# V's global rows straight into the copies' buffer, prices of the queue, jobs set into waits, and a first block in chunks of two tiles

## The chip, the cores and the metric

The kernel runs on one core of a Trainium2 chip. TensorE (PE in the profile, with PEld for its weight loads) multiplies matrices, VectorE (DVE), ScalarE (ACT) and GpSimd (POOL) work on elements, and SyncE (SP) issues the DMAs of this kernel in the order of its queue. The metric is the device time of one execution in microseconds (us): 894.03 us as the median of three runs, from 889.8 to 896.12.

## What is computed

Attention with a window, then two gated feed-forward blocks. The six weight matrices come as float64 and are turned into pairs of float16 parts on the chip; the rest is float32. There are 4 batches and 8 heads with 512 local and 32 global rows of 64 each:

```python
k_all = np.concatenate([k_g, k_l], axis=2); v_all = np.concatenate([v_g, v_l], axis=2)
out_g = np.matmul(sm(scale * np.matmul(q_g, k_all.transpose(0, 1, 3, 2))), v_all)
s_ll  = np.where(np.abs(pos[:, None] - pos[None, :]) <= 32, scale * q_l @ k_l.T, -1e9)
s_l   = np.concatenate([scale * q_l @ k_g.T, s_ll], axis=-1)
out_l = np.matmul(sm(s_l), v_all)
x  = np.concatenate([out_g, out_l], axis=2)          # as 2176 tokens x 512
xn = x / np.sqrt(np.mean(x * x, -1, keepdims=True) + 1e-6) * rms_g
x  = (silu(xn @ w_gate) * (xn @ w_val)) @ w_out      # 512 x 1536 and back
out = (sigmoid(x @ w2_gate) * (x @ w2_val)) @ w2_out
```

(Each local row sees the 32 global rows and the local ones at most 32 away; "@" with transposes is written short here.)

## The kernel before

**Attention.** The local rows are 16 tiles T of 128 rows, four to a batch. Per tile, q and k are loaded and transposed on PE (steps `q`, `k`), scores are made (`a1`, two score banks), the smallest is taken (`mx`, DVE), exponentials follow (`ex`, ACT), they are transposed (`a2`, PE), copied (`pc`) and multiplied with V (`a3`, 64 small matmuls per tile), normalized (`nm`), scaled (`sq`, `ms`, `sc`), split into two float16 parts in the tile `xs` (`xh`, `xm`) and sent by a transposing DMA to `xhi`, the input of the feed-forward block (`xl`, on SP). Once per batch the global rows go through `sg`, `g1`, `g2`, `g3`, `gx`.

**V's copies.** `a3` reads V from one of two buffers `vw0`, `vw1` (line 856; tile T uses `vw[T % 2]`), each with four blocks of rows: the row blocks that a 32-row strip of queries can see, and the global rows in the place that is left. `vw_pieces` (line 903) lists the copies of a tile: two large ones of 64 partitions, four small ones of 32, and for the first two tiles of a batch four more with the global rows. The buffer may only be written when `a3` of tile T-2 has read it. V's tile `vt` (six buffers) and V's global rows `vg` are loaded by `load_v` and `load_vg` (line 889), the latter four times into four strips of one tile; `st_vw` makes the copy on POOL, DVE, or as a DMA within SBUF on SP. A column of ones stands behind every head's 64 columns for the sum of the weights.

**Feed-forward.** The 17 row tiles (16 local, one of all global rows) go through block g=0 and g=1 of `w_gate`, `w_val` and `w_out` in chunks: `first` (line 1314) lists them as six chunks of three tiles (the last of two), that is of 384 columns and one of 256. A chunk takes 48 matmuls for gate and value (called GV here) when its tiles' `xl` have landed, and 24 for the output (OUT) one chunk later. Later blocks work on all rows at once and come after the attention.

**What sets the order.** The program is written by a list scheduler in the kernel itself. Every operation is a `task` with engines, a priority out of the table `PR` (line 1198) and the tasks that it depends on; `Booked` (line 88) prices each instruction as it is written, on a clock per engine in `now`, and `choose` (line 1435) takes the engine that is free first by these prices. A DMA's price on SP stands in line 123: 1250 ns for a transpose, 620 or 560 for others. `attend` (line 1493) runs this as long as attention tasks are left, with the chunks' matmuls as `G` pieces between them (`gemm`, line 1362); if PE has a gap of more than `fill` ns by these prices, it writes dummy matmuls on `ident` into it. From then on the order is that of the loops at the end, and `give` hands out conversion of weights and other side jobs to DVE, ACT and POOL at every `tick`. Nearly all instructions are recorded by the helper in line 145, so the rows of the profile carry that line and are told apart by their tiles.

Of the kernel before, what the change touches and what calls it, by code (L numbers as in the profile page):

```python
# [10 lines left out]
F32 = mybir.dt.float32  # L11
# [10 lines left out]
def tile_attention_moe_moe(  # L22
# [64 lines left out]

    class Booked:
# [4 lines left out]
        def __getattr__(self, name):  # L93
            f = getattr(self.eng, name)

            def g(*args, **kw):
# [3 lines left out]
                ins = [x for x in aps if x is not out]  # L100
                n = max(int(np.prod(x.shape[1:])) for x in aps) if "axis" in kw else int(np.prod(out.shape[1:]))
# [11 lines left out]
                elif key == "s":  # L113
# [9 lines left out]
                    now["s"] = t + (1250 if kw.get("transpose") else 620 if ns[0] < 100000 else 560 + 0.11 * min(max(now["dma"] - t, 0), 6000))  # L123
# [56 lines left out]
    SG = q_g.shape[2]  # L180
# [909 lines left out]
    def st_xh(T, e):  # L1090
        xs_t[T] = ap.tile([128, 2, DM], F16, tag="xs", name="xs", bufs=1)
# [42 lines left out]
    def st_g3(b, e):  # L1134
# [3 lines left out]
        for r in range(5):  # L1138
            for pr in range(NPR):
# [3 lines left out]
                else:  # L1143
                    l, v = pt[0:SG, r, 32 * pr:32 * pr + 32], vg[0:SG, h * DV:h * DV + D]
# [47 lines left out]
    def warm(n):  # L1192
        p = bank()
        for i in range(n):
# [3 lines left out]
    PR = dict(lkg=-7.25, kgt=7.41, lqg=-1.98, qgt=3.21, gB=1.07, lk=-4.25, lq=-1.55, lv=-0.02, lg=-0.66,  # L1198
              q=3.87, qc=-16.93, k=0.24, k0=-8.51, nk=-2.48, kc=3.82, kc0=-0.72, a1=8.55, vw=0.09, e=2.04,
              mx=-5.17, ex=2.53, a2=-3.33, pc=-0.11, a3=-0.84, nm=-4.07, sq=15.55, ms=-7.09, sc=-0.86,  # L1200
              a4=-18.55, xh=5.81, xl=-8.54, sg=8.94, g=5.82, lv0=-0.76, lk1=-6.39, G=1000, post=-7.94,
              raw=-3.21, w0=0.24, w1=0.35, w2=12.08, w3=16.91, w4=17.64, w5=-6.83, w6=7.76, w7=26.25,
              w8=11.55, Le=146, Ld=62, La=106, Lp=5314538, Ls=1690, backlog=4477, fill=1035, guard=1, kcd=0,
              land=1190, vs0=24309, vs1=341, vs2=1815, xt=0.37)
# [27 lines left out]
    def tile_tasks(T):  # L1232
# [6 lines left out]
        if t == 0:  # L1239
            task(("lg", b), "s", lambda e: load_vg(b), P(PR["lg"]),  # L1240
                 *([("vw", T - 8 + i, n) for i in range(2) for n in range(6, 10)] + [("g3", b - 2, 1)] if b >= 2 else []), after=ref("lg", b - 1))
# [32 lines left out]
        task(("xh", T), "ad", lambda e: st_xh(T, e), P("xh"), ("sc", T), ref("xl", T - 1), c=(520, 341))  # L1274
# [20 lines left out]

    def build_tasks():
        for n, a, dst in (("kg", k_g, kgT), ("qg", q_g, qgT)):
# [12 lines left out]
        task(("xh", NT), "ad", lambda e: st_xh(NT, e), NT, ("sc", NT), ref("xl", NT - 1), c=(520, 341))  # L1310
# [359 lines left out]
```

## Time and profile before

| | us |
|---|---|
| median of three runs | 894.03 |
| the profiled execution | 896.37 |
| its span, first to last instruction | 894.5 |
| PE busy in the span | 866.8 |
| DVE, ACT, POOL busy | 610.6, 452.2, 266.7 |

The profile is of one execution. Its span is 1.9 us shorter than the time of that execution, which is 2.3 us over the median of the runs. [...] The attention stage fills about the first 180 us.

### The profile page before, as it was taken

The page shows a single profiled execution, that of the slowest core. Times are in us where ns is not written, and L with a number is a line of the kernel's source. Part 1 is how long each engine was busy: PE and PEld are TensorE (multiplying, and loading weights), DVE is VectorE, ACT ScalarE, POOL GpSimd, SP SyncE. Part 2 cuts the span into 40 slices and gives each one's busy share as a digit, 9 for nine tenths or more (in the row PEclk, how much of TensorE's full clock was granted, in tenths as well). Part 3 has the DMA queues.
Part 4 walks back from the last instruction along what each step waited for, and adds up shares of the span by engine and source line. Part 5 has one row for each costly group of instructions (what it writes and reads, how often), then busy time and mean ns, then how long its engine had stood idle before and what let it go on. Part 6 is the DMA issues. An engine that isn't in the chain of part 4 may idle for free.

```text
span 894.5 us, 18832 instructions
## 1 busy us (share of the span) xinstructions
PE 866.8 (97%) x7733; PEld 543.3 (61%) x7733; DVE 610.6 (68%) x1050; ACT 452.2 (51%) x986; POOL 266.7 (30%) x300
## 2 busy tenths in 40 slices
PE   8889798899999999999999999999999999999998
PEld 6667565666666666666666666556556565556553
DVE  4867767697788888788737877748764468645252
ACT  4886586565334445555527444546545264344230
POOL 2754445342211211121214446442202122212010
PEclk9999999999999999999999999999999999999999
DMA  9977879461000114131300121110331003000102
GB/s 211 170 153 145 172 151 185 117 139 63 1 25 23 50 46 124 54 107 48 95 1 1 56 88 48 48 48 28 114 106 37 1 24 95 1 1 13 59 33 98
DMA packets 108998, 66.56 MB, mean 74 GB/s; under 512 B 76912, under 2 KB 101488, under 8 KB 108912
## 3 DMA queue, kind: packets, MB, share of 16 engines
q1 hardware_dynamic: 108912, 65.36, 29.2%
q8 instruction: 61, 1.00, 0.5%
q14 instruction: 25, 0.20, 0.1%
HBM read 52.17 MB, written 4.46 MB: 63 GB/s over the span
## 4 chain that ended last, share of the span: by engine, by line
PE 80%; DMA 9%; DVE 4%; ACT 2%; SPq 1%; issue 1%; POOL 1%; DVEq 0%; ACTq 0%; POOLq 0%
PE p L145 66%; PE b L145 14%; DMA vt<-in_v_l_dram 3%; DMA xhi<-xs 2%; DMA q<-in_q_l_dram 1%; DMA vw<-vt 1%; SPq L145 1%; DVE wf L145 1%; DVE xs L145 1%; DMA k<-in_k_l_dram 1%; ACT s L145 1%; DMA vg<-in_v_g_dram 1%; DVE ya L145 0%; ACT pt L145 0%; DVE wc L145 0%
## 5 line engine op out<-in xcount | busy, mean ns | idle before, releaser
L145 PEld LDWEIGHTS <-wc 128*128 128x128 f16 x2556 | 250.1, 98 | 144.8 <-issue 1.4
L145 PE MATMUL p<-tt,wc 128*128 128x384 f16 (+1 forms) x1296 | 208.6, 317 | 0.6 <-ACT gv L145 0.4
L145 PE MATMUL p<-xhi,wc 128*128 128x384 f16 (+1 forms) x1260 | 205.2, 317 | 0.0
L145 POOL TENSOR_TENSOR h<-gv,h 128x384 f16<-128x384 f32 (+1 forms) x66 | 84.4, 1279 | 286.1 <-ACT h L145 274.1
L145 PE MATMUL p<-wo,h 128*128 128x512 f16 x612 | 133.4, 379 | 0.0
L145 ACT ACTIVATE gv<-p 128x384 f32<-128x384 f32 (+1 forms) x174 | 80.4, 469 | 76.0 <-PE p L145 69.6
L145 DVE SCALAR_TENSOR_TENSOR wf<-raw,wf 128x512 int32<-128x512 int32 x144 | 113.2, 794 | 2.2
L145 PEld LDWEIGHTS <-wo 128*128 128x128 f16 x864 | 84.3, 98 | 47.7 <-issue 0.2
L145 PEld LDWEIGHTS <-h 128*128 128x128 f16 x612 | 59.9, 98 | 71.1
L145 DVE SCALAR_TENSOR_TENSOR ya<-p,ya 128x384 f32<-128x384 f32 (+2 forms) x106 | 61.0, 581 | 54.7 <-PE p L145 53.9
L145 PE MATMUL b<-xhi,wgv 128*128 128x384 f16 (+1 forms) x576 | 93.3, 320 | 2.0 <-DMA xhi<-xs 2.0
L145 ACT ACTIVATE h<-gv 128x384 f16<-128x384 f32 (+3 forms) x93 | 54.7, 592 | 73.5 <-DVE gv L145 71.2
L145 DVE SCALAR_TENSOR_TENSOR gv<-gv 128x384 f32<-128x384 f32 (+3 forms) x81 | 66.7, 823 | 36.2 <-ACT gv L145 35.3
L145 PE MATMUL p<-h,wo 128*128 128x384 f16 (+1 forms) x576 | 90.0, 317 | 0.0
L145 DVE TENSOR_TENSOR gv<-p,gv 128x384 f32<-128x384 f32 (+1 forms) x108 | 55.4, 530 | 46.8 <-ACT gv L145 46.6
L145 PEld LDWEIGHTS <-wgv 128*128 128x128 f16 x576 | 56.2, 99 | 34.6 <-issue 1.8
L145 ACT ACTIVATE sa<-p 128x384 f32<-128x384 f32 (+1 forms) x54 | 24.7, 466 | 79.2 <-PE p L145 79.0
L145 ACT ACTIVATE wf<-raw 128x512 f32<-128x512 f32 x72 | 47.2, 671 | 27.9 <-DVE wc L145 13.5
L145 POOL COPY vw<-vt 64x1040 f32<-64x1040 f32 (+1 forms) x37 | 39.5, 1069 | 50.2 <-DMA vt<-in_v_l_dram 38.7
L145 POOL TENSOR_TENSOR sm<-wf 128x256 f32<-128x256 f32 x18 | 15.4, 858 | 119.9 <-DVE wc L145 87.3
L145 POOL TENSOR_TENSOR hlo<-t,hhi 128x384 f16<-128x384 f32 (+1 forms) x24 | 26.6, 1109 | 69.3 <-ACT hhi L145 69.1
L145 PE MATMUL b<-hhi,wo 128*128 128x384 f16 (+1 forms) x192 | 46.9, 317 | 0.0
(117 smaller groups left out, 1007.1 us busy)
## 6 DMA issues: line engine op xcount, KB each, us to landing
raw<-in_moe_w_gate_dram SPq DMA_DIRECT2D x24, 512.0 KB, 4.1
raw<-in_moe_w_val_dram SPq DMA_DIRECT2D x24, 512.0 KB, 3.7
raw<-in_moe_w_out_dram SPq DMA_DIRECT2D x24, 512.0 KB, 3.7
k<-in_k_l_dram SPq DMA_DIRECT2D x16, 256.0 KB, 3.9
q<-in_q_l_dram SPq DMA_DIRECT2D x16, 256.0 KB, 4.9
vt<-in_v_l_dram SPq DMA_DIRECT2D x16, 256.0 KB, 5.3
out_dram<-ya SPq DMA_DIRECT2D x16, 256.0 KB, 2.0
vw<-vt SPq DMA_DIRECT2D x54, 65.0 KB, 2.8
```

Of the source, the lines that this page charges most:

```text
L145: return f(*args, **kw)
```

## The change

1. **V's global rows.** The tasks that put them into `vw` (pieces 6 to 9 of the first two tiles of a batch) are now loads from DRAM on SP, each straight into its strip of `vw`, with no tile between; the ones behind the heads are written once at the start (`st_ones`). `vg` is loaded once per batch (for `g3` only) instead of four times, with one buffer instead of two.
2. **V's copies.** From the third tile on the other pieces may go to POOL, SP or DVE, before to POOL or SP.
3. **Queue's times.** The prices of an issue on SP are raised from 620 and 560 to 700 and 620 ns, that of a transpose from 1250 to 1600.
4. **`xs`** has two buffers instead of one.
5. **The table `PR`** is a new one, with `fill` at 11881 instead of 1035.
6. **Jobs in waits.** Behind the attention stage, every instruction for DVE or ACT that would wait by the prices first lets `fill_in` write side jobs that end before it.
7. **The first block** (g=0) takes the first six tiles in chunks of two: 256, 256, 256, then as before.

```diff
-                    now["s"] = t + (1250 if kw.get("transpose") else 620 if ns[0] < 100000 else 560 + 0.11 * min(max(now["dma"] - t, 0), 6000))
+                    now["s"] = t + (1600 if kw.get("transpose") else 700 if ns[0] < 100000 else 620 + 0.11 * min(max(now["dma"] - t, 0), 6000))
...
+                if key in "da" and between[0]:
+                    between[0](key, max([wrote.get(tag_of(x), 0.0) for x in ins] + [free0.get(out.tensor.name, 0.0)]))
...
     def load_vg(b):
-        vg_t[b] = ap.tile([128, H * DV], F32, tag="vg", name="vg", bufs=2)
-        nc.gpsimd.memset(vg_t[b].rearrange("p (h d) -> p h d", h=H)[:, :, D:DV], 1.0)
-        for i in range(4):
-            nc.sync.dma_start(out=vg_t[b][32 * i:32 * i + SG].rearrange("p (h d) -> p h d", h=H)[:, :, 0:D],
-                              in_=v_g[b].rearrange("h p d -> p h d"))
+        vg_t[b] = ap.tile([128, H, D], F32, tag="vg", name="vg", bufs=1)
+        nc.sync.dma_start(out=vg_t[b][0:SG], in_=v_g[b].rearrange("h p d -> p h d"))
...
     def vw_eng(T, n):
-        return "ps" if T > 1 else "pd"
+        return "s" if n >= 6 else "psd" if T > 1 else "pd"
...
     def st_vw(T, n, e):
         o, v, r, m = vw_pieces(T)[n]
-        i = (vg_t[T // TPB] if v is None else vt_t[v])[r]
+        if v is None:
+            nc.sync.dma_start(out=o.rearrange("p (h d) -> p h d", h=H)[:, :, 0:D], in_=v_g[T // TPB].rearrange("h p d -> p h d"))
+            return
+        i = vt_t[v][r]
...
-        xs_t[T] = ap.tile([128, 2, DM], F16, tag="xs", name="xs", bufs=1)
+        xs_t[T] = ap.tile([128, 2, DM], F16, tag="xs", name="xs", bufs=2)
...
-    PR = dict(lkg=-7.25, kgt=7.41, lqg=-1.98, qgt=3.21, gB=1.07, lk=-4.25, lq=-1.55, lv=-0.02, lg=-0.66,
+    PR = dict(lkg=-2.69, kgt=6.46, lqg=-1.68, qgt=4.3, gB=-0.15, lk=-5.41, lq=-3.32, lv=-2.95, lg=1.61,
...
-    first = [(g, T, n) for g in range(min(2, GS)) for T, n in ((0, 3), (3, 3), (6, 3), (9, 3), (12, 3), (15, 2))]
+    first = [(0, T, n) for T, n in ((0, 2), (2, 2), (4, 2), (6, 3), (9, 3), (12, 3), (15, 2))]
+    first += [(1, T, n) for T, n in ((0, 3), (3, 3), (6, 3), (9, 3), (12, 3), (15, 2))]
...
+    def fill_in(e, t):
+        while t > now[e] + 200:
+            for _, key, js, i in handout():
+                op = js[i][1][0] if js is jobs else js[0]
...
+                s = max([now[e], 0 if free else ready.get(key, 0)] + [wrote.get(tag_of(x), 0.0) for x in (ins() if ins else ())])
+                if s + took.get(f.__code__, 900) <= t + 250:
+                    take(key, js, i)
+                    break
...
         w_go[0] = True
+        between[0] = fill_in
```

**Counts.** On SP the loads of `vg` go from 16 to 4, the copies `vw<-vg` from 10 to 0, the copies `vw<-vt` from 54 to 34, and 32 loads `vw<-in_v_g_dram` are new. On POOL the copies into `vw` go from 56 to 41, on DVE from 8 to 21. On PE the 88 dummy matmuls go, 144 GV matmuls of 256 columns stand for 96 of 384, and 72 OUT matmuls of 256 columns for 48 of 384. Ahead of the last `a3` stand 210 GV and OUT matmuls of 384 columns before, and 192 of 256 and 48 of 384 now; 720 and 144 (384 and 256 columns) are the totals of before, 576 and 360 those of now.

**PE at the start** (`hhi` is a zeroed tile for warming up, `x` holds the global rows of k or q, `ident` against itself is a dummy). Before, behind the first 13 warm-up matmuls, the end of a run of 56 dummies and the start of the next of 21:

```order
L145 LDWEIGHTS ident
L145 MATMUL b<-ident 128x256
L145 MATMUL b<-ident,k 128x128 x4
L145 MATMUL b<-ident,x 128x128 x4
L145 LDWEIGHTS ident
L145 MATMUL b<-ident 128x256
```

Now, from the end of the warm-up to the first score step:

```order
L149 MATMUL b<-hhi 128x384
L149 MATMUL b<-ident,k 128x128 x12
L149 MATMUL b<-ident,q 128x128 x4
L149 MATMUL b<-ident,x 128x128 x4
L149 MATMUL b<-ident,k 128x128 x4
L149 LDWEIGHTS ident
L149 MATMUL b<-mask,ident 32x8x32
```

The dummies are gone, three k tiles are transposed at once and the global rows of k come behind the first q.

**SP around tile 4, the first of the second batch** (vw0 is its buffer; the transposes are those of tiles 1 and 2 in the piece of before, of tiles 1, 2 and 3 in that of now). Before:

```order
L145 DMA_TRANSPOSE xhi0_73<-xs_1053 128x8x128
L145 DMA vw0_85<-vt_995 32x520 x3
L145 DMA vw0_85<-vg_729 32x520
L145 DMA vw0_85<-vt_1083 32x520
L145 DMA vw1_86<-vt_995 32x520
L145 DMA vw1_86<-vt_1083 32x520 x2
L145 DMA_TRANSPOSE xhi0_73<-xs_1258 128x8x128
L145 DMA q_1367<-in_q_l_dram 128x8x64
L145 DMA vw1_86<-vg_729 32x520
```

Now:

```order
L149 DMA_TRANSPOSE xhi0_73<-xs_949 128x8x128
L149 DMA q_1061<-in_q_l_dram 128x8x64
L149 DMA vt_1080<-in_v_l_dram 128x8x64
L149 DMA_TRANSPOSE xhi0_73<-xs_1078 128x8x128
L149 DMA raw_1162<-in_moe_w_out_dram 128x1024
L149 DMA raw_1170<-in_moe_w_out_dram 128x1024
L149 DMA vw0_85<-in_v_g_dram 32x8x64
L149 DMA_TRANSPOSE xhi0_73<-xs_1185 128x8x128
L149 DMA vw0_85<-in_v_g_dram 32x8x64 x3
L149 DMA k_1328<-in_k_l_dram 128x8x64
```

The last pieces of tile 4's V stood ahead of tile 2's transpose; now its global rows stand behind the transposes of tiles 2 and 3 and behind two loads of `w_out`, which came later before.

**SP around tiles 12 and 13** (vw0 and vw1; V of tiles 13, 14 and 15 is in vt_2853, vt_3017 and vt_3134 before, in vt_2562, vt_2742 and vt_2958 now). Before:

```order
L145 DMA vw0_85<-vt_2853 32x520
L145 DMA vw1_86<-vt_2853 32x520 x2
L145 DMA raw_2985<-in_moe_w_gate_dram 128x4x256
L145 DMA raw_2988<-in_moe_w_gate_dram 128x4x256
L145 DMA vt_3017<-in_v_l_dram 128x8x64
L145 DMA_TRANSPOSE xhi1_74<-xs_2990 128x8x128
L145 DMA vw0_85<-vt_2853 32x520
L145 DMA raw_3117<-in_moe_w_val_dram 128x4x256
L145 DMA vt_3134<-in_v_l_dram 128x8x64
L145 DMA vw1_86<-vt_3017 32x520
```

Now:

```order
L149 DMA vw0_85<-in_v_g_dram 32x8x64 x2
L149 DMA vw1_86<-vt_2562 32x520
L149 DMA vw1_86<-vt_2742 32x520
L149 DMA q_2887<-in_q_l_dram 128x8x64
L149 DMA_TRANSPOSE xhi1_74<-xs_2885 128x8x128
L149 DMA vt_2958<-in_v_l_dram 128x8x64
L149 DMA vw1_86<-in_v_g_dram 32x8x64 x4
L149 DMA vw0_85<-vt_2742 32x520
L149 DMA vw0_85<-vt_2958 32x520
```

The last row of the piece of before, a copy for tile 13, is SP's 151st issue; the four loads for the same tile end with the 138th now, and the three weight loads that stood between come behind them.

## Rows read from the trace of the kernel before

**Rows 1.** The page's totals: busy us (share of the span) xinstructions per engine.

```profile
PE 866.8 (97%) x7733; PEld 543.3 (61%) x7733; DVE 610.6 (68%) x1050; ACT 452.2 (51%) x986; POOL 266.7 (30%) x300
```

**Rows 2.** Table of stretches: stretch in us, its length, busy us (instructions) per engine.

```profile
core 0: us, PE busy (x) PEld busy (x) DVE busy (x) ACT busy (x) POOL busy (x), PEclk, DMA share, GB/s
0.00:40.00 40.00, 34.81 (x643) 26.89 (x644) 26.81 (x50) 24.82 (x73) 18.58 (x49) 1.00 0.95 204
40.00:80.00 40.00, 36.17 (x956) 27.38 (x958) 27.49 (x69) 31.31 (x103) 24.75 (x41) 0.96 0.75 148
80.00:120.00 40.00, 34.25 (x689) 24.10 (x678) 26.69 (x55) 27.06 (x80) 17.44 (x26) 1.00 0.83 159
120.00:160.00 40.00, 33.09 (x760) 23.18 (x764) 28.52 (x63) 26.86 (x76) 21.17 (x32) 0.96 0.85 171
160.00:200.00 40.00, 38.23 (x467) 25.59 (x456) 32.74 (x60) 23.56 (x51) 16.74 (x18) 0.96 0.53 120
200.00:400.00 200.00, 199.79 (x1307) 127.63 (x1305) 165.72 (x304) 95.17 (x188) 40.90 (x39) 1.00 0.18 56
...
800.00:894.50 94.50, 90.78 (x520) 50.60 (x517) 36.04 (x59) 25.53 (x55) 9.49 (x8) 1.00 0.13 48
```

**Rows 3.** Waits of PE from 0 to 200 us: total us, times, longest.

```profile
PE b L145 <- DMA q<-in_q_l_dram: 6.3, 5, 2.6
PE b L145 <- DMA vw<-vt: 4.4, 5, 3.0
```

**Rows 4.** Waits of SP's queue from 0 to 164 us, in the same columns.

```profile
SPq L145 <- PE b L145: 25.8, 23, 2.8
```

**Rows 5.** Groups of PE's instructions by shape, 0 to 200 us: the dummies (busy us, mean ns).

```profile
L145 PE MATMUL b<-ident 128*128 128x256 bf16 x88 | 10.4, 275 | 0.2 <-ACT qT L145 0.2
```

**Rows 6.** Timeline of PE at the start: start us, us, what [idle before <-releaser].

```profile
19.09 0.63 PE L145 MATMUL b<-ident,k 128*128 128x128 f32 x4 [0.30 <-DMA k<-in_k_l_dram]
```

**Rows 7.** SP's issues by tile, 0 to 164 us: ns min/median/max, first and last start.

```profile
L145 SPq DMA_DIRECT2D raw<-in_moe_w_val_dram x4: 385/520/575, 5.3 to 156.4; - x4
L145 SPq DMA_DIRECT2D vg<-in_v_g_dram x16: 443/450/1880, 16.4 to 120.2; - x16
L145 SPq DMA_DIRECT2D vw<-vg x10: 534/611/3046, 57.1 to 137.5; - x10
L145 SPq DMA_DIRECT2D vw<-vt x54: 507/541/2257, 33.4 to 163.0; - x54
```

**Rows 8.** Timeline of PE: a3 of tile 13, and the end of the last a3.

```profile
159.65 1.62 PE L145 MATMUL b<-vw,pt 128*32 128x65 f32 x58 [3.00 <-DMA vw<-vt]
...
175.93 0.62 PE L145 MATMUL b<-vw,pt 128*32 128x65 f32 x20
```

**Rows 9.** Timeline of SP: the copy that tile 13 waits for is the first of these.

```profile
152.84 2.87 SPq L145 DMA_DIRECT2D vw<-vt  x2
```

**Rows 10.** Timeline of PE behind the attention: runs of 48 GV matmuls.

```profile
185.27 7.96 PE L145 MATMUL b<-xhi,wgv 128*128 128x384 f16 x48
...
198.08 5.41 PE L145 MATMUL b<-xhi,wgv 128*128 128x256 f16 x48 [0.95 <-DMA xhi<-xs]
```

**Rows 11.** DVE's copies into vw, 0 to 164 us: ns min/median/max.

```profile
L145 DVE COPY vw<-vt x5: 684/751/1549, 21.7 to 31.4; 32x520 f32<-32x520 f32 x3, 64x1040 f32<-64x1040 f32 x2
```

**Rows 12.** Groups of DVE's instructions, 0 to 200 us: busy us, mean ns, idle before.

```profile
L145 DVE CAST xs<-x 128x512 f16<-128x512 f32 x8 | 4.8, 602 | 8.3 <-DMA xhi<-xs 8.2
```

**Rows 13.** The page's DMA issues: count, KB each, median us from issue to landing.

```profile
vw<-vt SPq DMA_DIRECT2D x54, 65.0 KB, 2.8
vg<-in_v_g_dram SPq DMA_DIRECT2D x16, 64.0 KB, 3.4
```

**Rows 14.** Timeline of PE: end of a3 of tile 3, and a3 of tile 4.

```profile
55.45 1.07 PE L145 MATMUL b<-vw,pt 128*32 128x65 f32 x26
...
61.51 1.12 PE L145 MATMUL b<-vw,pt 128*32 128x65 f32 x64
```

**Rows 15.** Timeline of SP: the transpose of tile 3.

```profile
67.74 1.94 SPq L145 DMA_TRANSPOSE xhi<-xs  x1
```

More of the change, by code (lines that the diff above doesn't have):

```diff
@@ L1196, in warm @@
         now["e"] = 5300.0
-    PR = dict(lkg=-7.25, kgt=7.41, lqg=-1.98, qgt=3.21, gB=1.07, lk=-4.25, lq=-1.55, lv=-0.02, lg=-0.66,
[L1199 to L1204, printed above, removed]
+    PR = dict(lkg=-2.69, kgt=6.46, lqg=-1.68, qgt=4.3, gB=-0.15, lk=-5.41, lq=-3.32, lv=-2.95, lg=1.61,
+              q=8.79, qc=-19.63, k=-0.6, k0=-6.65, nk=-4.99, kc=-5.28, kc0=-5.62, a1=3.42, vw=-1.33, e=6.5,
+              mx=-5.27, ex=4.41, a2=-12.53, pc=-1.44, a3=-4.3, nm=-10.83, sq=12.88, ms=-5.39, sc=-2.57,
+              xh=2.11, xl=-6.63, sg=1.46, g=-1.73, lv0=2, lk1=0.62, G=1000, post=-18.5, raw=-4.44, w0=-0.14,
+              w1=0.41, w2=7.51, w3=18.35, w4=22.01, w5=-4.2, w6=18.4, w7=26.17, w8=12.84, Le=0, Ld=0, La=136,
+              Lp=17005804, Ls=1305738, backlog=2127, fill=11881, guard=1, kcd=0, land=2310, vs0=17142,
+              vs1=384, xt=-8.9, vd=306.21, vz=-0.52)
     class Task:
@@ L1240, in tile_tasks @@
             task(("lg", b), "s", lambda e: load_vg(b), P(PR["lg"]),
-                 *([("vw", T - 8 + i, n) for i in range(2) for n in range(6, 10)] + [("g3", b - 2, 1)] if b >= 2 else []), after=ref("lg", b - 1))
+                 *([("g3", b - 1, 0), ("g3", b - 1, 1)] if b else []), after=ref("lg", b - 1))
         task(("q", T), "e", lambda e: tr4(("q", T), q_t.pop(T).rearrange("p h d -> p (h d)"), ("qc", T)), P(PR["q"]), ("lq", T), ref("a1", T - 2) if PR["guard"] else None, banks=1)
@@ L1294, in batch_tasks, with st_ones @@
         task(("gxc", b), "ad", lambda e: st_gxc(b, e), P(8), ("gx", b), c=(525, 607))
+    def st_ones():
+        for w in vw:
+            nc.gpsimd.memset(w.rearrange("p i (h d) -> p (i h) d", d=DV)[:, :, D:DV], 1.0)
     def build_tasks():
+        task(("ones",), "p", lambda e: st_ones(), PR["k0"])
         for n, a, dst in (("kg", k_g, kgT), ("qg", q_g, qgT)):
@@ L1541, in fits, with handout, take @@
         return free or ready.get(key, 0) <= t
+    took = {}
     def run_op(key, op):
         e, f = (op.eng, op.f) if isinstance(op, Op) else (op[0] and op[0].lower(), op[1])
-        f()
+        t = e and now[e]
+        b, between[0] = between[0], None
+        f()
+        between[0] = b
+        if e:
+            took[f.__code__] = now[e] - t
         if e:
             ready[key] = now[e] + 130
+    def handout():
+        c = []
+        for a in (0, 2, 1):
+            if part_jobs[a]:
+                c.append((0.0, f"h{a}", part_jobs[a], 0))
+        for key, ops in (("c", c_ops), ("s", s_ops)):
+            if ops:
+                c.append((due_w(ops), key, ops, 0))
+        for k in range(2):
+            i = [i for i, x in enumerate(jobs) if x[0][1] == k]
+            if i:
+                key = jobs[i[0]][0]
+                if k == 0 or not any(x[0] == (key[0], 0) for x in jobs):
+                    c.append((due_j(key), key, jobs, i[0]))
+        return sorted(c, key=lambda x: x[0])
+    def take(key, js, i):
+        op = js[i][1].pop(0) if js is jobs else js.pop(0)
+        if js is jobs and not js[i][1]:
+            js.pop(i)
+        run_op(key, op)
+    def fill_in(e, t):
+        while t > now[e] + 200:
+            for _, key, js, i in handout():
+                op = js[i][1][0] if js is jobs else js[0]
+                eng, ins, free, f = (op.eng, op.ins, op.free, op.f) if isinstance(op, Op) else (op[0] and op[0].lower(), None, op[0] == "A", op[1])
+                if eng != e or key[0] == "h" or isinstance(op, Op) and op.ok and not op.ok():
+                    continue
+                s = max([now[e], 0 if free else ready.get(key, 0)] + [wrote.get(tag_of(x), 0.0) for x in (ins() if ins else ())])
+                if s + took.get(f.__code__, 900) <= t + 250:
+                    take(key, js, i)
+                    break
+            else:
+                return
     def give():
@@ L1551, in give @@
             w_give()
[L1552 to L1574 removed]
+            for _, key, js, i in handout():
+                if fits(key, js[i][1][0] if js is jobs else js[0]):
+                    take(key, js, i)
                     break
```

38 lines of the change are left out of this document (9 added, 29 removed).

## Prediction

> **What bounds the kernel now.** Read the totals first, then the stretches, then who waits for whom. TensorE (PE) is busy for 866.8 of 894.5 us [rows 1], so the question is where the other 27.7 us lie. The table of stretches answers it [rows 2]: from 0 to 200 us PE is busy for 34.81 + 36.17 + 34.25 + 33.09 + 38.23 = 176.55 us, so 23.45 us are idle; from 200 to 400 us it is busy for 199.79 of 200, and the last stretch loses 3.7 us, behind the last matmul. After the attention stage the kernel is PE's work and nothing else. The time can therefore be written as: when the last step a3 (probabilities times V) of the attention ends, plus the matmuls still to be done then, plus a constant.
>
> In those 200 us PE's named waits are first of all for DMAs: 6.3 us for q tiles and 4.4 us for the vw buffers [rows 3]. Both are issued by SyncE's queue (SP), which works in order. SP in turn waits 25.8 us for PE [rows 4], because a vw buffer, a k and a q tile are only overwritten when PE has read them. So the stage is a loop of PE and SP: PE waits for what SP sends, SP for what PE frees, and neither is full. The DMA engines are 75 to 95% busy there [rows 2], near their limit but not at it. A saving counts if it makes SP's queue shorter ahead of the last tiles.
>
> **Startup: 82 of the 88 filler matmuls go.** With the new table fill=11881 no gap is thought long enough, and all 88 vanish from PE's order. They were 10.4 us of busy time [rows 5], but that is no gain by itself: they stand in front of steps that wait for a DMA, as the fourth k tile's transposes at 19.09 us [rows 6]. The bound is 0 to -10.4 us. What starts the first score step is the fourth k tile, SP's 17th issue before and the 13th now; four issues at 0.45 us [rows 7] are 1.8 us. But the first a3 needs V rows that are the 27th issue before and now. I take 0. What the fillers may have bought is the clock: the granted clock was 1.00 from 0 to 40 us and 0.96 from 40 to 80, 120 to 160 and 160 to 200 us [rows 2], about 0.04 x 40 = 1.6 us of full speed each time. Without fillers one or two such falls may come in the first 20 us, at 1.6 us each; the 82 fillers there leave 10.4 x 82/88 = 9.7 us of spare, so this too I put at 0, with up to 3 us for the range.
>
> [...]
>
> **SP's queue up to tile 13.** The last wait of PE for vw is the one of 3.00 us before the a3 of tile 13 [rows 8]; from its end, 159.65 + 1.62 = 161.27 us, to the end of the last a3 at 175.93 + 0.62 = 176.55 us little is idle (1.8 us from 160 to 200 us [rows 2], of which 0.95 come later). So tile 13's vw is the point at which the queue stops mattering. By the order, the copy it waits for is SP's 151st issue, at 152.84 us [rows 9], and the 138th in the changed kernel. The 13 fewer are: raw weights 9 to 6, loads of vg 16 to 3, copies vw<-vg 10 to 0, copies vw<-vt 47 to 28, against 32 new loads of V's global rows straight into vw. At the medians [rows 7]: 3 x 0.52 + 13 x 0.45 + 10 x 0.61 + 19 x 0.54 - 32 x 0.45 = 1.6 + 5.9 + 6.1 + 10.3 - 14.4 = 9.4 us (a new load is priced as the old load of vg, the same 64 KB in the same rows). The upper end is the queue's pace with its waits, 152.84 / 151 = 1.01 us an issue, or 13.2 us; the lower is 0, if only the waits for PE set the pace. I take 9.4, the part that surely leaves the queue. Between that a3 and the last one PE does 36 GEMM matmuls before and 30 now, 1.0 us less. The last a3 comes 10.4 us earlier.
>
> **What is left to do then.** By PE's order 210 GEMM matmuls of 384 columns lie ahead of the last a3; in the changed kernel 192 of 256 columns and 48 of 384. A run of 48 takes 7.96 us at 384 columns (0.166 each) and 5.41 us at 256 (0.113) [rows 10]. Done ahead: 34.8 us before, 21.6 + 8.0 = 29.6 now. All of it: 720 x 0.166 + 144 x 0.113 = 135.6 before, 576 x 0.166 + 360 x 0.113 = 136.1 now; the smaller chunks cost 0.5 us in all. Left: 100.8 and 106.5, so +5.7 us. With more to do, PE no longer reaches the final chunk ahead of its transposes: the 0.95 us it waits for them at 198.08 us [rows 10] go.
>
> **Edits at nothing.** VectorE (DVE) makes 21 copies into vw instead of 8: 13 x 0.75 = 9.8 us [rows 11]. It is busy for 26 to 29 of every 40 us up to 160 us [rows 2], so there is room, and it loses waits: the second xs buffer takes away 8.2 us in which DVE stood still until a transpose had read the first [rows 12]. If the room is not where it is needed, the difference of 1.6 us is the price. GpSimd makes 41 copies instead of 56. The new filling of waits behind the attention stage works on DVE and ScalarE where PE idles for 0.21 us in 200 [rows 2]; there is nothing to win, and up to 1 us to lose.
>
> **Sum.** -10.4 + 5.7 - 0.95 = -5.65 us. The profiled execution took 896.4 us, so 890.7; the median of the runs is 894.03, 2.3 lower, so 888.4 is forecast.
>
> **Rivals.** A is the sum: 888.4, from 884.6 (pace of 13.2 us) to 893.1 (half of the 9.4).
>
> B: the table's truer queue times also put PE's steps where their data has come. For it: the new price of a transpose's issue, 1600 ns for 1250, is nearer to the 1.94 us of [rows 15]. Half of PE's waits for q and vw, 5.4 us, and half of the three falls of the clock, 2.4 us, come on top: 880.6. Against it: one loop of PE and SP remains, with as many vw buffers.
>
> C: the DMA engines, not the queue, set the pace. At a share of 0.95 they moved 204 GB/s [rows 2], 215 at full, so 64 KB take 0.30 us. 20 more loads from DRAM cost 6.1 us; 30 fewer copies within SBUF give back something from nothing to 9.1; three weight loads of 512 KB moved back give 7.3. With nothing for the copies the stage is 1.2 us shorter instead of 9.4: 888.4 + 8.2 = 896.6. The new loads also land later, 3.4 against 2.8 us [rows 13]. Against it: shares of 0.83 and 0.85 in 80 to 160 us.
>
> [...]
>
> D, the other side: the new loads stand behind transposes in SP's queue. In tile 4's turn three of the four loads of vw's global rows now follow tile 3's transpose. That transpose was issued at 67.74 us, 11.2 us after tile 3's a3 had ended at 56.52 [rows 14, 15]; with 1.94 us of its own, three issues of 0.45 and 3.4 to land, tile 4's a3 could start 17.9 us after tile 3's. PE has 72 GEMM matmuls of 256 columns there, 8.1 us, and the 5.0 us of attention steps that fill 56.52 to 61.51 now [rows 14]. 4.8 us are missing. For tiles 8 and 12 one and two loads stand behind the transposes of tiles 6 and 10; if these come as late, three places cost 14.4 us, or 902.8. It decides at tile 4 if the transpose comes later than 6.4 us behind the a3. Against it: the second xs buffer shortens just this chain, and the two later places have a tile more of distance.
>
> **Chances.** A 0.50, B 0.22, C 0.16, D 0.12. A measurement of this kernel tells about 1% from no change, so faster is below 885.1 and slower above 903.0. Faster: B with most of its weight and a sixth of A, 0.30. Slower: D, 0.12. The same: 0.58. The range 878 to 900 leaves out D and the lower quarter of B, nearly 0.2; A's own is 884.6 to 893.1.
>
> **What would show it.** PE's last a3 near 166 us; tile 13's a3 without its 3 us wait, and its vw issued near 143 us; no wait for the transposes before the 256-column run of 48; no filler, and a lower clock ahead of 20 us at most. The forecast is wrong if the last a3 ends later than 172 us (then the 5.7 us of work left behind eat the gain), if tile 4's a3 waits several us for vw (D), or if PE idles behind 200 us.

## The result and the profile after

The changed kernel takes 881.68 us (median of 4 runs, 879.96 to 882.75), the kernel before beside it 893.38 us. The ratio is 0.987, with a 95% interval of 0.983 to 0.9909: faster by 1.3%, or 11.7 us. The forecast was 888.4, that is 0.9937 of the 894.03 from which it was worked out, above the interval. Rival B's 880.6 (0.985) lies in it, and so close to the measured time that the text below asks first whether B's reason was the right one too. By the prediction's own line (faster is below 885.1 us) the change is faster, which had a chance of 0.30; "the same" had 0.58. Taken a second time, beside the last three experiments, the changed kernel had 879.34 us and 0.9873 (0.9849 to 0.9897).

The page's totals after, in the columns of [rows 1]:

```profile
span 878.2 us, 18796 instructions
...
PE 854.1 (97%) x7717; PEld 541.0 (62%) x7717; DVE 619.1 (70%) x1063; ACT 451.3 (51%) x995; POOL 254.1 (29%) x286
```

The profiled execution took 879.96 us, 1.7 below the median, where the one of before was 2.3 above it. So the two traces differ by 16.3 us of span, of which the medians bear out 11.7. The table of stretches after, in the columns of [rows 2]:

```profile
0.00:40.00 40.00, 27.74 (x518) 19.45 (x518) 24.76 (x45) 22.83 (x67) 12.64 (x44) 0.83 0.98 199
40.00:80.00 40.00, 37.70 (x926) 30.83 (x924) 35.41 (x77) 31.32 (x100) 23.73 (x36) 1.00 0.92 180
80.00:120.00 40.00, 37.53 (x1033) 31.22 (x1023) 33.12 (x78) 33.31 (x108) 24.09 (x37) 1.00 0.95 167
120.00:160.00 40.00, 39.00 (x861) 29.35 (x861) 35.27 (x82) 31.58 (x89) 14.34 (x24) 1.00 0.69 159
160.00:200.00 40.00, 40.00 (x271) 26.41 (x270) 35.47 (x57) 24.47 (x47) 12.71 (x13) 1.00 0.46 119
...
400.00:800.00 400.00, 397.81 (x2422) 236.80 (x2421) 261.81 (x382) 196.66 (x369) 117.67 (x90) 1.00 0.15 45
```

In 40 to 160 us PE is busy for 114.2 us of 120; in [rows 2] it was 103.5. The lower clock stands in the first 40 us alone. The three falls of before, to half the clock for 3.41 us each, are gone; they began at 54.22, 139.56 and 160.03 us, within 0.9 us of the ends of waits of PE of 1.49, 2.64 and 3.00 us. Who waits for whom, of PE and of SP's queue from 0 to 200 us, in the columns of [rows 3] and [rows 4]:

```profile
PE b L149 <- DMA k<-in_k_l_dram: 7.2, 2, 4.0
PE b L149 <- issue: 3.1, 3, 1.1
...
PE b L149 <- DMA q<-in_q_l_dram: 0.5, 1, 0.5
PE b L149 <- DMA vw<-vt: 0.3, 1, 0.3
PE b L149 <- DMA vw<-in_v_g_dram: 0.3, 1, 0.3
PE b L149 <- DMA xhi<-xs: 0.2, 1, 0.2
...
SPq L149 <- PE b L149: 14.1, 25, 1.7
```

PE's waits for q and vw, 10.7 us before, are 1.1 us; SP waits for PE 14.1 us instead of 25.8. The timeline of PE shows three places: tile 4's a3, tile 13's a3 (in two parts) and the end of the last a3:

```profile
69.70 1.34 PE L149 MATMUL b<-vw,pt 128*32 128x65 f32 x64
...
138.39 0.66 PE L149 MATMUL b<-vw,pt 128*32 128x65 f32 x32
...
140.50 0.67 PE L149 MATMUL b<-vw,pt 128*32 128x65 f32 x32
...
153.81 0.53 PE L149 MATMUL b<-vw,pt 128*32 128x65 f32 x24
```

The last a3 ends at 153.81 + 0.53 = 154.34 us, 22.2 us earlier than before [rows 8]; the forecast said 10.4. Where these 22.2 us were can be read from one stretch in each trace, from 40 us to the last a3 (first row: all of PE; second and third: only instructions with the tile wgv, and with wo, which are the GEMM). Before:

```profile
40.00:176.55 136.55, 119.24 (x2696) 86.34 (x2695) 93.67 (x215) 93.47 (x276) 69.69 (x103) 0.96 0.77 154
...
40.00:176.55 136.55, 29.72 (x163) 15.92 (x164) 1.22 (x1) 1.06 (x1) 0.96 0.77 154
...
40.00:176.55 136.55, 8.97 (x48) 4.45 (x48) 1.23 (x1) 1.06 (x1) 0.96 0.77 154
```

After:

```profile
40.00:154.34 114.34, 108.57 (x2762) 87.23 (x2761) 98.61 (x227) 91.17 (x282) 58.67 (x92) 1.00 0.87 170
...
40.00:154.34 114.34, 26.50 (x192) 18.25 (x192) 0.00 (x0) 0.00 (x0) 1.00 0.87 170
...
40.00:154.34 114.34, 6.46 (x49) 4.68 (x50) 1.23 (x1) 1.06 (x1) 1.00 0.87 170
```

| us from 40 to the last a3 | before | after | difference |
|---|---|---|---|
| GEMM (wgv and wo) | 38.7 | 33.0 | -5.7 |
| other work of PE | 80.5 | 75.6 | -4.9 |
| PE idle | 17.3 | 5.8 | -11.5 |
| sum | 136.55 | 114.34 | -22.2 |

The other work is nearly the same matmuls (2485 and 2521 records), so its 4.9 us are the clock: three falls of 3.41 us at half speed make 5.1. The 5.7 us of GEMM are not won, they come later. The gain in this stretch is idle time and clock, 16.4 us, and it is the whole gain: behind the last a3 the span has 723.86 us, before 717.95, which is 5.91 more.

### The profile page after: what moved, and what is told of

It is laid out like the page before. It is cut to its first block, busy times and chain, and to the rows that moved or that the text cites. A ratio compares the mean times of both kernels' runs of the same rounds, so it can differ in the third digit from the quotient of the medians.

```text
span 878.2 us, 18796 instructions
## 1 busy us (share of the span) xinstructions
PE 854.1 (97%) x7717; PEld 541.0 (62%) x7717; DVE 619.1 (70%) x1063; ACT 451.3 (51%) x995; POOL 254.1 (29%) x286
## 4 chain that ended last, share of the span: by engine, by line
PE 89%; DVE 3%; ACT 3%; DMA 2%; issue 1%; POOL 1%; SPq 0%; POOLq 0%; DVEq 0%; ACTq 0%
PE p L149 67%; PE b L149 22%; DVE gv L149 1%; DVE wf L149 1%; DMA xhi<-xs 1%; DMA q<-in_q_l_dram 1%; DMA vw<-vt 0%; SPq L149 0%; DMA vw<-in_v_g_dram 0%; DVE xhi L149 0%; ACT kTr L149 0%; ACT pt L149 0%; DVE gmx L149 0%; DVE wc L149 0%; ACT h L149 0%
## 5 line engine op out<-in xcount | busy, mean ns | idle before, releaser
L149 POOL TENSOR_TENSOR h<-gv,h 128x384 f16<-128x384 f32 (+1 forms) x66 | 86.2, 1307 | 304.2 <-ACT h L149 289.4
L149 PEld LDWEIGHTS <-wo 128*128 128x128 f16 x888 | 86.7, 98 | 46.1 <-issue 0.2
L149 DVE SCALAR_TENSOR_TENSOR wf<-raw,wf 128x512 int32<-128x512 int32 x144 | 107.6, 755 | 2.0
L149 DVE SCALAR_TENSOR_TENSOR gv<-gv 128x384 f32<-128x384 f32 (+3 forms) x81 | 70.5, 870 | 42.7 <-ACT gv L149 41.9
L149 PEld LDWEIGHTS <-wgv 128*128 128x128 f16 x624 | 60.5, 98 | 28.2 <-issue 1.5
L149 POOL TENSOR_TENSOR sm<-wf 128x256 f32<-128x256 f32 x18 | 16.2, 901 | 108.4 <-DVE wc L149 76.3
L149 POOL COPY vw<-vt 64x1040 f32<-64x1040 f32 (+1 forms) x41 | 37.9, 923 | 24.1 <-PE b L149 11.8
```

The lines of the kernel that those rows point to most:

```text
L149: return f(*args, **kw)
```

## The experiments

Two theories stood against each other. The **queue theory** is the sum of the prediction: SP's queue is shorter, and the other edits are worth nothing. The **order theory** (B): PE's steps now stand where their data has come, and each part of the change feeds that. Ratios are to the kernel before on the same chip; the change itself has 0.987. A trace shows one execution of each run, so differences of a few tenths of a us between traces say nothing: the two profiles of the changed kernel end their last a3 at 154.34 and 153.69 us. One thing holds for all experiments that undo a part: the list scheduler then writes another order for the whole attention, with a table of priorities that was not made for it. Where an order was held, it is said.

**e1: the first block in chunks of three tiles again.**

```diff
-    first = [(0, T, n) for T, n in ((0, 2), (2, 2), (4, 2), (6, 3), (9, 3), (12, 3), (15, 2))]
-    first += [(1, T, n) for T, n in ((0, 3), ...
+    first = [(g, T, n) for g in range(min(2, GS)) for T, n in ((0, 3), (3, 3), (6, 3), ...
```

> The changed kernel with the first block in chunks of three tiles again; table, prices, V's path, xs and jobs in waits as changed (the scheduler writes a new order). Queue theory (the gain comes from SP's shorter queue and its truer prices): the chunks matter little, PE has less to do while it waits in the first 60 us but 0.5 us less to do in all: the changed kernel's 881.7 us within 2 us. Chunk theory (PE fills the waits of the attention because the first matmuls of the block can start after two transposes instead of three): about 5 us slower, 887, with PE idle between 50 and 75 us.

Measured: 888.08 us, 0.9958 (0.9937 to 0.9979). The last a3 ends at 157.21, 2.9 us later than in the changed kernel, PE is idle for 4.5 us more until then, and 6.0 us more lie behind it. GEMM can only start when a whole chunk's tiles are through: here its first matmul starts at 61.2 us, with chunks of two at 57.4, and PE has spent 4.5 us less on it by the last a3 (28.5 instead of 33.0 us busy). About 1.7 us of the 6.0 behind are a fall of the clock (0.92 and 0.91 in 470 to 480 and 480 to 490 us) that the changed kernel's profile does not have. I had given the chunks a price (+0.5 us) and no gain.

**e3: one xs buffer again.**

```diff
-        xs_t[T] = ap.tile([128, 2, DM], F16, tag="xs", name="xs", bufs=2)
+        xs_t[T] = ap.tile([128, 2, DM], F16, tag="xs", name="xs", bufs=1)
...
-        task(("xh", T), ..., ref("xl", T - 2), c=(520, 341))
+        task(("xh", T), ..., ref("xl", T - 1), c=(520, 341))
```

> The changed kernel with one xs buffer instead of two (and the task that waits for it as before). Queue theory: the 8.2 us in which DVE stood still for transposes come back but lie beside other work: 882 to 884. xs theory (these waits sat in front of the steps that PE and SP wait for): 887 to 890, with DVE waiting several us for xhi<-xs.

Measured: 889.62 us, 0.9964 (0.9944 to 0.9985); last a3 at 158.42, 4.1 us later. The profiled execution was the fastest of ten (884.86 us, mean granted clock 0.990); seven of them took 889.3 to 891.0 us at 0.982 to 0.985, so the trace shows only a part of the median's loss, and the rest goes with a lower clock. The buffer that I had put at nothing for PE is worth several us in this order.

**e13: V's copies on GpSimd and SP alone.**

```diff
-        return "s" if n >= 6 else "psd" if T > 1 else "pd"
+        return "s" if n >= 6 else "ps" if T > 1 else "pd"
```

> The changed kernel, but V's local rows of the tiles from the second on are copied by GpSimd or by SP's queue alone, as before, not by VectorE too. If the queue binds, SP has up to 13 to 19 copies more at 0.54 us, and the last a3 comes 5 to 10 us later than 154.3: 884 to 889 us, ratio 0.990 to 0.996. If GpSimd takes them at no cost, the last a3 stays within 2 us of 154.3 and the ratio at 0.985 to 0.989.

Measured: 881.99 us, 0.9897 (0.987 to 0.9924), beside 879.34 for the changed kernel on the same chip: 2.65 us. The last a3 ends at 156.37, 2.0 to 2.7 us later than in the two profiles of the changed kernel. That is between the two expectations, and the smallest of the parts; the two intervals overlap. SP makes 42 copies of V here instead of 34, and eight issues at the 0.25 us that e8 finds (below) are an estimate of 2.0 us, about what is seen.

**e4 and e5: the prices of SP's issues.** e4 is the changed kernel with the old prices, e5 the kernel before with the new ones and nothing else.

```diff
-  now["s"] = t + (1600 if kw.get("transpose") else 700 if ns[0] < 100000 else 620 + 0.11 * ...
+  now["s"] = t + (1250 if kw.get("transpose") else 620 if ns[0] < 100000 else 560 + 0.11 * ...
```

> The changed kernel, its new table included, with the old prices of an issue (620, 560 and 1250 ns). Order theory (the truer prices put PE's steps where their data has come): PE's waits for q and vw, 0.8 us in the changed kernel and 10.7 before, come back in half or more, SP waits longer for PE: 887 to 892. Queue theory (the shorter queue alone carries the gain): 881 to 884.

> The kernel before with the new prices of an issue alone, its old table kept. Order theory: truer prices by themselves put PE's steps later and nearer to their data: 5 us faster or more, ratio 0.993 or less. Queue theory: no issue is saved, so ratio 0.997 to 1.003. A table that was searched for the old prices may also lose by it: ratio over 1.003, and then prices and table only work as a pair.

Measured: e4 892.41 us, 1.0002 (0.9983 to 1.0021): with every other part in place the gain is gone, and the last a3 comes at 161.54, 7.2 us later, with 4.8 us more behind it. But the waits do not bear out the reason that the expectation gave. PE's waits for q and vw stay at 0.8 us, SP waits for PE 15.9 us (14.1 in the changed kernel), and what grows is idle time of PE before which the profile shows no releaser (0 to 200 us):

```profile
PE b L149 <- issue: 8.1, 8, 2.5
```

In the changed kernel these are 3.1 us. SP also has 42 copies `vw<-vt` again instead of 34, an estimated 2.0 us at e8's 0.25 us an issue. So e4 shows what the prices are worth in this program, not that they act through PE's waits for q and vw.

e5 887.26 us, 0.9945 (0.9917 to 0.9974): three numbers alone bring 4.6 us, between what the two theories had put. Its last a3 ends at 166.83 us, where the forecast had put that of the whole change. The waits of e5, of PE and of SP's queue from 0 to 200 us:

```profile
PE b L145 <- DMA q<-in_q_l_dram: 5.8, 5, 3.3
PE b L145 <- DMA vw<-vt: 1.7, 3, 1.0
...
SPq L145 <- PE b L145: 21.3, 26, 2.6
```

The wait for vw fell from 4.4 to 1.7 us. The new prices also sent eight copies into vw from SP to other engines (238 issues in the whole program instead of 246), so the queue is a little shorter too; at the 0.25 us that e8 finds for an issue these are 2 of the 9.7 us by which the last a3 is earlier. This trace also has one fall of the clock (3.41 us at half) fewer than that of before. The rest goes with the new order, and fits B only in part: PE's waits for q and vw together fell from 10.7 to 7.5 us.

Nor are the new prices nearer to the durations in every way. The plain issues of [rows 7] have medians of 450 to 611 ns, so 700 and 620 ns are farther off than 620 and 560. The mean of all plain issues up to 164 us is 784 ns, that of the transposes 1795 (median 1528): the new prices are nearer to the means, which hold the long rows too.

**e10: the kernel before with the new prices and the new table.**

```diff
-    PR = dict(lkg=-7.25, kgt=7.41, ... land=1190, vs0=24309, vs1=341, vs2=1815, xt=0.37)
+    PR = dict(lkg=-2.69, kgt=6.46, ... land=2310, vs0=17142, vs1=384, xt=-8.9, ..., vs2=1815)
```

> The kernel before with two things of the change: the new table of priorities and the new prices of SP's issues; V's global rows still go over vg and GpSimd, xs has one buffer, the first block goes in chunks of three. If the table and the prices alone carry the gain, the ratio to the kernel before is 0.987 to 0.991 and the last a3 ends near 156 us. If the parts need each other (a table is worth something only for the program that it was made for), it is no better than with the prices alone, 0.9945, and more likely 1.0 or above, the last a3 behind 167 us. My expectation is the second.

Measured: 893.37 us, 1.002 (1.0001 to 1.0038); last a3 at 175.31. The table without the parts for which it was made takes back what the prices gave. One place can be named, V's global rows at the start:

```profile
L145 SPq DMA_DIRECT2D vg<-in_v_g_dram x4: 448/450/1041, 32.8 to 34.8; - x4
```

In the kernel before and in e5 these loads begin at 16.4 and 16.2 us. The new table puts them late (`lg` is 1.61 instead of -0.66), which fits a program where `vg` serves `g3` alone; by the old path the first a3 needs them. It starts at 41.25 us instead of 32.70 in e5, and from there to the end of the last a3 both take 134.1 us. So the 8.5 us that e10 loses against e5 at the last a3 are there at the first one; that this one entry costs them was not tried by itself. No wait of PE for q or vw is listed in e10, and yet it is no faster than the kernel before: those waits alone do not set the time. SP's queue waits for PE longer than in any other kernel here (0 to 200 us):

```profile
SPq L145 <- PE b L145: 36.9, 40, 3.2
```

**e8: 32 more issues, with the order held.** Each load of V's global rows is split in two: the same bytes, the same order on every engine, 32 more DMAs on SP's queue.

```diff
-            nc.sync.dma_start(out=ov, in_=iv)
+            booked_only(ov, iv)
+            raw_dma(out=ov[:, 0:4], in_=iv[:, 0:4])
+            raw_dma(out=ov[:, 4:8], in_=iv[:, 4:8])
```

> The changed kernel with its order held on every engine, but each of the 32 loads of V's global rows on SP issued as two of half the heads: 32 more issues, the same bytes and the same 256-byte rows. If SP's own issue time bounds the attention (queue theory), 32 x 0.45 = 14 us more work in the queue move the last a3 by 8 to 14 us: 889 to 896. If the DMA engines bound it (they are 92 to 98% busy up to 120 us in the changed kernel), nothing is added for them: 881 to 884.

Measured: 890.32 us, 0.9983 (0.9969 to 0.9998). The last a3 ends at 162.29, 8.0 us later, and behind it lie 723.8 us as in the changed kernel. So 32 issues cost 8.0 us there, 0.25 us each, the fall of the clock named below included. PE's waits from 0 to 200 us:

```profile
PE b L149 <- DMA vw<-in_v_g_dram: 3.6, 3, 2.4
PE b L149 <- DMA q<-in_q_l_dram: 1.5, 3, 0.8
...
PE b L149 <- DMA vw<-vt: 1.4, 4, 0.7
```

And a stretch of its table:

```profile
80.00:120.00 40.00, 37.20 (x928) 30.82 (x933) 31.90 (x75) 31.52 (x101) 23.43 (x37) 0.96 0.84 159
```

PE again waits for vw and q, 6.5 us instead of 1.1, and a fall of the clock is back (103.56 to 106.97 us). The DMA engines' share in this stretch fell from 0.95 to 0.84 and the kernel became slower: here SP's issues bind, not the engines' bandwidth. A half load's row on SP is 0.43 us in the median, a whole one's was 0.45, and of each added row 0.25 us arrived at the end of the attention.

**e6: V's global rows by the old path** (into vg, one buffer of it, and copies into vw on GpSimd, VectorE or SP).

```diff
-        vg_t[b] = ap.tile([128, H, D], F32, tag="vg", name="vg", bufs=1)
-        nc.sync.dma_start(out=vg_t[b][0:SG], in_=v_g[b].rearrange("h p d -> p h d"))
+        vg_t[b] = ap.tile([128, H * DV], F32, tag="vg", name="vg", bufs=1)
+        for i in range(4):
+            nc.sync.dma_start(out=vg_t[b][32 * i:32 * i + SG]...
...
-        return "s" if n >= 6 else "psd" if T > 1 else "pd"
+        return "psd" if T > 1 else "pd"
```

> The changed kernel with V's global rows by the old path: four loads of vg per batch and copies on POOL, SP or DVE (vg with one buffer, since the second xs buffer takes its place). Queue theory: the issues of the copies come back to the queue or to POOL and DVE, at 9.4 us by the prediction: ratio 0.995 to 1.0. If the direct loads are worth nothing and table, prices and chunks carry the gain: ratio 0.985 to 0.990.

Measured: 903.55 us, 1.0114 (1.0078 to 1.015), slower than the kernel before. The first a3 starts at 42.72 us instead of 32.76, the last ends at 178.24, and behind the start the clock is at half from 57.5 to 60.9, from 142.9 to 146.3 and from 153.1 to 159.9 us. This run is confounded: it has one vg buffer beside two of xs, where before had two beside one. The second xs buffer stands in the place of vg's second one, which the old path used; so this run doesn't give the price of the direct loads alone. The 10.0 us at the first a3 are not the buffer's doing, since only one load of `vg` has been made by then: as in e10, its four DMAs come late, from 34.1 us on.

**e7 and e11: does the lost clock at the start cost anything?** e7 puts 72 idle matmuls into PE's first three waits, with the order held.

```diff
+        for i in range({("k", 1): 36, ("k", 2): 28, ("q", 0): 8}.get(key, 0)):
+            one = ident.bitcast(BF16)
+            tc.nc.tensor.matmul(p[:, 0:256], one[:, 0:128], one, start=True, stop=True)
```

> The changed kernel with its order held, and 72 dummy matmuls on ident set into PE's first three waits for k and q tiles (36, 28 and 8, about 0.11 us each), which stay inside the waits of 4.0 and 3.1 us seen there. Clock theory: the granted clock stays 1.00 instead of 0.50 from 10 to 24 us, the first a3 (32.8 us) starts 1 to 3 us earlier and the time falls by 1 to 4 us, ratio 0.983 to 0.986. Cover theory (the prediction's): PE waits there anyway, ratio within 0.001 of the changed kernel's 0.987.

Measured: 881.29 us, 0.9863 (0.983 to 0.9897), no difference that can be told. The start of the changed kernel in PE's timeline:

```profile
5.24 1.06 PE L149 MATMUL b<-ident,k 128*128 128x128 f32 x4
10.31 1.11 PE L149 MATMUL b<-ident,k 128*128 128x128 f32 x4 [4.01 <-DMA k<-in_k_l_dram]
14.57 0.69 PE L149 MATMUL b<-ident,k 128*128 128x128 f32 x2 [3.15 <-DMA k<-in_k_l_dram]
```

And in its table of stretches (the granted clock is the third number from the right):

```profile
0.00:10.00 10.00, 5.20 (x17) 2.68 (x17) 2.38 (x6) 3.31 (x6) 2.60 (x20) 1.00 0.72 210
10.00:24.00 14.00, 8.85 (x98) 6.34 (x99) 8.24 (x12) 6.67 (x17) 2.33 (x10) 0.51 1.21 212
24.00:40.00 16.00, 13.69 (x405) 10.43 (x403) 14.14 (x29) 12.85 (x44) 7.71 (x14) 1.00 0.94 180
```

And that of e7:

```profile
0.00:40.00 40.00, 32.17 (x651) 24.33 (x654) 26.14 (x48) 24.43 (x70) 13.40 (x45) 1.00 0.97 203
```

The clock is at 1.00 throughout, the first a3 starts 2.05 us earlier (30.71), and the last ends 0.76 us earlier (153.58), or 0.11 earlier than in the second profile of the changed kernel. In e7's other three runs the mean granted clock was 0.994 to 0.996, so they had falls somewhere; the changed kernel's four had 0.990 to 0.992. A start at half the clock, 14 us long, is nearly hidden; that the steps behind it wait for SP's loads anyway is the likely reason, not shown here.

e11 adds to that the removal of `fill_in` (e2, next).

> The changed kernel without the filling of waits behind the attention stage, and with 72 idle matmuls of 256 columns in PE's first three waits, which hold the clock up. If the two are independent, the wait of 2.0 us of PE near 468 us is gone and the clock stays at 1.00 from the start: span 875 to 877 us, ratio 0.981 to 0.984, as without the filling alone. If the filling was worth something that the clock hides, 0.985 or more.

Measured: 879.24 us, 0.9867 (0.9845 to 0.9889), beside 879.34 for the changed kernel on the same chip: the same. Here the 72 matmuls did not hold the clock; two stretches of its table:

```profile
20.00:40.00 20.00, 14.74 (x396) 11.23 (x401) 13.87 (x27) 12.43 (x43) 8.52 (x20) 0.85 0.87 177
40.00:60.00 20.00, 18.91 (x499) 14.72 (x484) 15.24 (x38) 15.38 (x52) 9.87 (x18) 0.89 0.69 148
```

It fell at 20.42 and at 37.49 us, and the last a3 ended at 156.10, 1.8 to 2.4 us later than in the two profiles of the changed kernel.

**e2: without the filling of waits behind the attention stage.**

```diff
-        between[0] = fill_in
```

> The changed kernel without the filling of waits behind the attention stage; PE's order is the same row for row. Queue and order theory: PE is full there anyway, so within 2 us of the changed kernel (ratio to the kernel before 0.985 to 0.989). If the one wait of 2.0 us of PE for ScalarE's gv near 468 us, which the kernel before does not have, comes from a side job that fill_in put ahead, it goes and the time falls by 1 to 2 us.

Measured: 877.24 us, 0.9826 (0.9783 to 0.9869), the lowest time of all. PE's order is that of the changed kernel. In the changed kernel PE has one wait behind 200 us that counts; its rows and those of ACT and DVE around it:

```profile
466.72 0.84 PE L149 MATMUL p<-tt,wc 128*128 128x320 f16 x5
469.60 0.57 PE L149 MATMUL p<-tt,wc 128*128 128x320 f16 x3 [2.04 <-ACT gv L149]
...
468.33 0.83 ACT L149 ACTIVATE tt<-ya 128x768 f16<-128x768 f32 x1
469.11 0.77 ACT L149 ACTIVATE gv<-p 128x320 f32<-128x320 f32 x2
...
467.79 0.68 DVE L149 TENSOR_SCALAR wf<-wf 128x1024 int32<-128x1024 int32 x1
468.46 0.56 DVE L149 TENSOR_TENSOR h<-gv,h 128x384 f16<-128x384 f32 x1
```

The same place in e2:

```profile
466.85 2.33 PE L149 MATMUL p<-tt,wc 128*128 128x320 f16 x16 [0.20 <-ACT gv L149]
...
466.36 0.77 ACT L149 ACTIVATE gv<-p 128x320 f32<-128x320 f32 x2 [0.70 <-DVE h L149]
467.01 0.84 ACT L149 ACTIVATE tt<-ya 128x768 f16<-128x768 f32 x1
```

With the filling, DVE converts weights (0.68 us) ahead of `h`, and ACT makes a `tt` (0.83 us) ahead of the copy of `p` for which PE stands; without it both come behind. The span behind the last a3 is 722.45 us in e2 and 722.2 in e11, against 723.86 and 723.81 in the two profiles of the changed kernel and 723.8 in e7 and e8, which have the filling too. So the filling costs 1.4 to 1.6 us, by four traces with it and two without. In the times themselves it is not settled: the intervals of e2 and of the change overlap, and e11, beside the changed kernel, lost as much at its start.

**The changed kernel again**, beside e10, e11 and e13.

> The changed kernel as it is, beside the other three on the same chip, so that the version without the filling of waits can be compared with it: 880 to 883 us, ratio 0.985 to 0.989, with a wait of 2.0 us of PE near 468 us. If the filling costs what that wait is, it stays 2 us or more above the version without it.

Measured: 879.34 us (5 runs, 879.11 to 880.72), 0.9873 (0.9849 to 0.9897); last a3 at 153.69, and the wait of 2.0 us is there again.

## Why the prediction was half right

The time lies in the stated range of 878 to 900, but not in A's own (884.6 to 893.1): the range held it because it was drawn to take in most of B. That B's 880.6 came so near is in part luck. It counted half of PE's waits and half of the falls; in the two traces nearly all of both went, and the medians bear out only 11.7 of the traces' 16.3 us.

**What held.** The form of the sum was right: the end of the last a3, and the work left behind it. The work left grew by 5.91 us, forecast 5.7 - 0.95 = 4.75; of the 1.2 over it, the filling's 1.4 to 1.6 are more than all. The 0.95 us wait for transposes is gone; the run of 48 starts without one. A new load of V's global rows takes SP 0.454 us in the median, priced at 0.45. The start's price of 0 held, though the clock did not go as put: no filler, but a fall from 10 to 24 us, 6.9 us of full speed, where 20 us was to be the end of it and 3 us the most. The first a3 starts at 32.76 instead of 31.62, and between the traces of e7 and the change no more than 0.76 us reach the last a3.

**C and D fell.** C: the DMA share rose to 0.92 to 0.98 up to 120 us, and yet behind 40 us no wait of PE for a load is longer than 0.5 us; e8 became slower at a lower share. D: tile 4's a3 starts at 69.70 us with no wait. It was close. The timeline of SP there:

```profile
61.66 1.49 SPq L149 DMA_TRANSPOSE xhi<-xs  x1
63.20 1.62 SPq L149 DMA_DIRECT2D vw<-in_v_g_dram  x3
```

The transpose comes 6.65 us behind tile 3's a3 (end at 55.01), just past the 6.4 that I had named as the limit; the loads are issued by 64.82 and land in 4.0 us by the page's median, at 68.8, 0.9 us before tile 4 needs them.

**The step that failed: what a shorter queue does to the loop.** I priced the queue by the issues that leave it, 9.4 us, and called PE's remaining waits those of "one loop of PE and SP", which stay. Tile 13's loads were to be issued near 143 us and the last a3 to end near 166. Measured, SP's loads of V's global rows up to 164 us, in the columns of [rows 7]; tile 13's are the last four:

```profile
L149 SPq DMA_DIRECT2D vw<-in_v_g_dram x32: 427/454/1848, 23.1 to 134.7; - x32
```

SP's 138th issue is at 134.7 us; in [rows 9] the 151st was at 152.84, so 13 fewer issues go with 18.1 us. The upper bound of the sum, the queue's pace of 1.01 us an issue, gave 13.2, and the pace itself got a little quicker (134.7 / 138 = 0.98). I chose the lower value, "the part that surely leaves the queue", since the rest of the pace was SP's waits for PE. But these fell as well, from 25.8 to 14.1 us: 9.4 of issues and 11.7 of waits make 21.1, about what was measured at tile 13 (its a3 comes 21.3 us earlier) and at the last a3 (22.2 instead of 10.4). This is a match of sums and no proof. SP's rows themselves, added up one by one as far as these two issues, make 131.0 and 114.5 us, which is 16.5 us less, and the gaps between them 21.9 and 20.1. So the term was mis-sized: at medians it took 9.4 us for rows that shrank by 16.5. How much of a long row is waiting, the traces do not tell. In PE's account the 11.8 us that were missed are 6.3 of idle time (11.5 instead of the 5.2 that the sum implies, 10.4 less 5.2 of GEMM) and 4.9 of clock. B held half of PE's waits and half of the falls to be at stake and got 0.22; nearly all of both went.

Fewer issues are hardly the whole reason. By e8 one is worth 0.25 us at the last a3, so 13 would bring about 3 us; this is an estimate, as e8 added issues to the new order and took none from the old one. There SP's waits took up a part of what was added (7.8 us for PE instead of 14.1). What the runs show beside it: the scheduler's prices are worth 4.6 us in the old program and the whole gain in the new one (e5 and e4), though by which waits stays open; the new table loses at its start what it may win later where V's global rows go the old way (e10); and the chunks of two and the second xs buffer, which I had put at a cost or at nothing, belong to the order that works (e1, e3). Undone, by the ratios, the prices cost 1.3%, the chunks 0.9%, xs 0.9%, VectorE's copies 0.2 to 0.3% (with overlapping intervals): 3.3% together where the change brought 1.3%. So these numbers are not shares of the gain; each also holds the cost of a table that no longer fits.

**The size of the clock.** The profiled execution of before showed three falls. Its mean granted clock was 0.994; over 15 runs of before beside the repeat it went from 0.994 to 1.00. So part of the 4.9 us belongs to that one execution, and this is a part of why the traces differ by 16.3 us and the medians by 11.7. The changed kernel's profile was the better one of its runs too: 0.992, where its other three had 0.990. Its mean clock is thus lower than that of before, and it is faster all the same, since its low stretch lies at the start, where e7 finds it to cost little (0.76 us or less at the last a3). I had costed the three falls rightly, but had taken them for a property of the kernel.

**The filling** was given nothing to win and up to 1 us to lose. It lost 1.4 to 1.6.

**What stays open.** Which of PE's waits the prices remove: with the old ones back (e4) the time is lost and the waits for q and vw are not. How much the new loads of the global rows are worth with the order held: e6 is confounded by vg's buffer, and neither part was tried alone in the old order. Whether the changed kernel without `fill_in` is faster in time, as it is in the trace.

## What to carry to other kernels

When a scheduler writes the order, try its prices early: three changed numbers brought 4.6 us with nearly the same work. Compare them with the means of the profile's rows as well as the medians, since a queue's long rows count too (here a mean of 784 ns beside medians of 450 to 611). A table of priorities belongs to the program that it was made for: one entry that is harmless there can hold up the first step of another. In a loop where PE waits for a queue and the queue for PE, don't price the issues that are removed alone: ask how much of both waits can go, and with them falls of the clock, which in the trace of before began near the ends of waits of 1.49 to 3.00 us. A wait that is gone is not yet time won (e10). A buffer or a smaller chunk that seems to win nothing where it stands may be what lets the next engine's work arrive in time; and filling idle engines with side jobs can put these jobs ahead of the copy for which the busy engine waits.

## What the runs showed of the hardware

An added issue on SP's queue, 0.43 us in the median, arrived with 0.25 us at the end of the attention (e8), although the bytes were the same and the DMA engines less busy than before the split (0.84 instead of 0.95 in 80 to 120 us). Half the bytes made a load's row hardly shorter: 0.43 us instead of 0.45. The granted clock was 0.51 from 10 to 24 us in the changed kernel, where waits of PE of 4.01 and 3.15 us end at 10.31 and 14.57 us; this cost 0.76 us or less at the end of the attention (e7). With 72 idle matmuls in PE's first waits it stayed at 1.00 in the profile of e7, but its other three runs had a mean of 0.994 to 0.996, and with the same matmuls it fell at 20.42 and 37.49 us in the profile of e11. No run here shows what number of idle matmuls keeps such a fall away.
